# Order of SP's value loads and of POOL's second-sketch read for the last batch, in a polysketch attention and feed-forward kernel

## The chip, the cores and the metric

The kernel runs on one core of a Trainium2 chip. The metric is the device time of one execution in microseconds (us). The engines are named as in the profile: PE (TensorE), DVE (VectorE), ACT (ScalarE), POOL (GpSimd) and SP (SyncE, which here only issues transfers). Each engine works through its own list of instructions in order; what it waits for are semaphores that other engines or landed transfers raise.

## The reference

Four batches with four heads, a sequence of 1088, head dimension 32, sketch size 8; then a feed-forward layer with a squared ReLU over all 4352 tokens (d_model 128, d_ff 2048).

```
def phi(x):
    a = einsum('rd,bhsd->bhsr', S1, x)
    b = einsum('rd,bhsd->bhsr', S2, x)
    return einsum('bhsi,bhsj->bhsij', a, b).reshape(*x.shape[:-1], 64)
q_p, k_p = phi(q), phi(k)
kv  = einsum('bhsf,bhsd->bhfd', k_p, v);  z = sum(k_p, axis=2)
num = einsum('bhsf,bhfd->bhsd', q_p, kv)
den = einsum('bhsf,bhf->bhs', q_p, z)[..., None] + 1e-06
x   = (num / den) as (4352, 128)
out = square(maximum(x @ w_in, 0)) @ w_out
```

The feature map phi of a row is the outer product of two sketches of it, the first with S1, the second with S2: 8 x 8 = 64 features a head.

## The kernel before

The work is cut into 578 named operations, each a few instructions on one engine. A string, PLAN, holds all of them in one order written out in full, as `name:engine:buffers`; what an engine runs, it runs in the order in which its operations stand in PLAN. Waits follow from the data and the buffers that operations share.

Names carry the batch and a part. For batch b:

- **Loads** (on SP): ldk, ldq and ldv bring K, Q and V. V of one batch comes in five pieces, ldvb.0 to ldvb.4 (L494): four of 128 KB into `vin`, one small one into `vtl`. The weights come on POOL: w_in0, w_out0, w_in1, w_out1, w_in2, w_out2 (L377, L382), after a small copy called gate that waits for a value load.
- **Keys and values**: tk transposes K (DVE), ksk makes both sketches (PE), kr brings them into rows (DVE, L583), kp multiplies them to features (DVE, L591), vp copies V into rows with a one behind them (POOL, L527 and L530), kv multiplies features and values (PE, L654), in parts kvb.0 and kvb.1; vpb.0 needs all four large pieces of V. kve brings the result out of PSUM.
- **Queries of batches 0 and 1**: tq transposes (DVE), qr makes replicated sketches (PE, L727), qa and qp copy and multiply them (ACT L749, DVE L763), num, mx, tx and xe make the quotient and lay it out as x.
- **Queries of batches 2 and 3**: qr (PE, L859) makes both sketches of all heads, ab copies them to the tile `ab` (ACT). The denominator is worked out first, from zm, zt, zk, zb, dt and dr (DVE and PE); dx spreads its reciprocal (POOL, L891), and da (DVE, L896 and L897) multiplies it into the first sketch. The sketches are then written to a scratch tensor `scr` in device memory, each in four transfers on SP (L903): wrb.1.0 to wrb.1.3 is the second sketch, wrb.0.0 to wrb.0.3 the first, with the denominator in it. They are read back, spread over 128 partitions, in two halves of the sequence (0 and 544): rdA (SP, L918, two transfers) brings the first sketch into `qp`, rdB (L925, four transfers) the second into `Bq`, on POOL, but for rdB3.544 on SP. All halves are 544 KB. qp (DVE, L965) multiplies the two, num (PE, L982) makes x, xe copies it out of PSUM (L995).
- **Feed-forward**: ten stages n of 256 or 512 tokens. For each pair m of column tiles of d_ff: m1.n.m (PE, L1094) multiplies x by w_in, r.n.m takes the ReLU (ACT L1104, some on DVE L1106), g.n.m squares (DVE L1114, some on ACT L1112), m2.n.m (PE, L1128) adds the product with w_out. oe.n transposes the result (DVE, L1153; the last stage copies it, L1139), and four stores a stage and batch, st n.token.quarter, go out on SP (L1163, the last at L1144).
- **Heat** operations are matmuls of zeros ahead of the real work.

Stages of the feed-forward run between the attention of later batches: stages 1 to 4 are at work while batches 2 and 3 are prepared, and stage 6 needs xe3.0. Three PSUM tiles h0 to h2 of two banks each are shared by m1, sketches and num; four tiles r0 to r3 and four g0 to g3 hold what r and g make.

The SP list around the change, from PLAN with the other engines left out:

```
ldk3.0 ldv3.1 ldv3.4 ldq3.0 wr2.1.1 wr2.1.3 st0.0.0 wr2.1.2 wr2.1.0 ldv3.0 st1.256.3 ldv3.2 ldv3.3
wr2.0.0 wr2.0.3 wr2.0.2 wr2.0.1 rdA2.0 wr3.1.2 st2.768.3 wr3.1.1 rdA2.544 wr3.1.3 st1.256.1 wr3.1.0
st0.0.2 wr3.0.2 wr3.0.3 wr3.0.1 wr3.0.0 rdA3.0 rdA3.544 st3.1280.3 st2.1088.1 rdB3.544 ...
```

and the whole POOL list:

```
mk2 iota zc z0 SR gate vp0.0 kp0.7 w_in0 w_out0 w_in1 w_out1 w_in2 w_out2 S64 SKw z1 vp1.1 vp1.0
vp2.1 vp2.0 rdB2.0 dx2 vp3.0 vp3.1 rdB2.544 dx3 rdB3.0
```

mk2, iota, zc, z0, z1, SR, S64 and SKw are small constants and arranged sketch matrices; ident and zr on DVE are an identity and its sums.

Of the kernel before, what the change touches and what calls it, by code (L numbers as in the profile page):

```python
# [40 lines left out]
zero:DVE mk2:POOL ldk0.0:SP mkz:DVE mk:DVE S1:SP heat0:PE:o0 iota:POOL ident:DVE zr:DVE zc:POOL heat1:PE:o0 heat2:PE:o0 z0:POOL tk0.0:DVE heat3:PE:o0
heat4:PE:o0 heat5:PE:o0 heat6:PE:o0 S0:ACT ST:DVE SK:DVE ldk0.1:SP ldk0.2:SP tk0.1:DVE ldq0.0:SP heat7:PE:o0 ksk0.0:PE:a0 tq0.0:DVE ldv0.0:SP
ka0.0:ACT kp0.0:DVE ksk0.1:PE:h2.1 ka0.1:ACT kp0.4:DVE SR:POOL qr0.0:PE:h1.1:h1.0 qa0.0.0:ACT:A0 heat8:PE:o0 heat9:PE:o0 qp0.0.0:DVE ldv0.1:SP
ldv0.2:SP qa0.0.1:ACT:A1 ldv0.3:SP ldv0.4:SP ldq0.8:SP ldq1.0:SP heat10:PE:o0 heat11:PE:o0 heat12:PE:o0 gate:POOL qp0.0.1:DVE vp0.0:POOL kv0.0:PE:h0.1
ldk1.0:SP tq0.8:DVE qr0.1:PE:h2:h1 tq0.24:DVE kp0.7:POOL w_in0:POOL vp0.1:ACT qa0.1.1:ACT:A2 qp0.1.1:DVE qa0.1.0:ACT:A0 kv0.1:PE kv0.2:PE heat13:PE:o0
w_out0:POOL kve0.0:DVE num0.0:PE:a0 tq1.0:DVE w_in1:POOL qp0.1.0:DVE w_out1:POOL kve0.1:ACT kve0.2:ACT w_in2:POOL w_out2:POOL mx0.0:DVE:den0 tk1.1:DVE
qr0.2:PE:h1:h0 qa0.2.0:ACT:A1 qa0.2.1:ACT:A2 heat14:PE:o0 qp0.2.0:DVE num0.1:PE:h2 tx0.0:PE:a0 xe0.0:ACT S64:POOL heat15:PE:o0 heat16:PE:o0 ldv1.1:SP
tk1.0:DVE qp0.2.1:DVE mx0.1:DVE:den1 m1.0.0:PE:h1 r.0.0:ACT:r0 ksk1:PE:h0 heat17:PE:o0 g.0.0:ACT:g0 m1.0.1:PE:h1 r.0.1:ACT:r1 tx0.1:PE:a0 SKw:POOL
kr1:DVE kp1.4:DVE qr1.0:PE:h2:h0 ldv1.2:SP qa1.0.0:ACT:A0 qp1.0.0:DVE qa1.0.1:ACT:A1 xe0.1:ACT heat18:PE:o0 m2.0.0:PE:o0 m1.0.2:PE:h1 r.0.2:ACT:r2
g.0.1:DVE:g1 ldv1.3:SP ldv1.4:SP ldv1.0:SP ldk2.0:SP z1:POOL m1.0.3:PE:h2 r.0.3:ACT:r3 num0.2:PE:a0 tq1.12:DVE m1.1.4:PE:h1 m2.0.1:PE ldq2.0:SP  # L50
r.1.4:ACT:r0 m1.1.0:PE:h2 r.1.0:ACT:r1 g.0.2:DVE:g2 mx0.2:DVE:den2 g.0.3:DVE:g3 qp1.0.1:DVE m2.0.2:PE kp1.0:DVE vp1.1:POOL m1.1.1:PE:h1 tx0.2:PE:a0
xe0.2:DVE m2.0.3:PE r.1.1:ACT:r2 g.1.1:DVE:g0 ldv2.0:SP qr1.1:PE:h0:h2 vp1.0:POOL g.1.4:DVE:g1 m1.1.3:PE:h1 g.1.0:ACT:g2 ldv2.4:SP qa1.1.1:ACT:A2
r.1.3:ACT:r3 ldv2.1:SP kv1.0:PE:a0 oe0:DVE:osb0 qp1.1.1:DVE kv1.1:PE m1.1.2:PE:h1 m2.1.0:PE:o0 qa1.1.0:ACT:A0 m1.1.5:PE:h2 tq2.0:DVE qp1.1.0:DVE
st0.0.1:SP tk2.0:DVE ldv2.2:SP tk2.1:DVE kve1.0:ACT kve1.1:ACT m2.1.1:PE ldv2.3:SP r.1.2:ACT:r1 kve1.2:ACT g.1.2:DVE:g3 r.1.5:ACT:r2 m1.1.7:PE:h0
g.1.5:ACT:g2 vp2.1:POOL ldk3.0:SP num1.0:PE:a0 mx1.0:DVE:den0 qr2:PE:h1 ksk2:PE:h2 ldv3.1:SP tx1.0:PE:a0 ldv3.4:SP ldq3.0:SP r.1.7:ACT:r0 g.1.3:DVE:g0
m1.1.6:PE:h0 ab2:ACT wr2.1.1:SP xe1.0:ACT m2.1.2:PE r.1.6:ACT:r1 m1.2.3:PE:h1 wr2.1.3:SP r.2.3:ACT:r2 st0.0.0:SP kr2:DVE kp2.0:DVE g.1.7:ACT:g3
kp2.4:DVE m2.1.3:PE m1.2.4:PE:h2 r.2.4:ACT:r3 tk3.0:DVE vp2.0:POOL kv2.0:PE:a0 tk3.1:DVE qr1.2:PE:h0:h1 wr2.1.2:SP kv2.1:PE zm2:DVE wr2.1.0:SP
m2.1.4:PE qa1.2.0:ACT:A1 qp1.2.0:DVE zt2:PE:h2.1 zk2:DVE m2.1.5:PE qa1.2.1:ACT:A2 m1.2.0:PE:h0 g.1.6:ACT:g0 m2.1.6:PE m1.2.1:PE:h2 m2.1.7:PE ldv3.0:SP
qp1.2.1:DVE kve2:ACT zb2:PE:a0 r.2.0:ACT:r0 rdB2.0:POOL tq3.0:DVE g.2.0:ACT:g1 oe1:DVE:osb1 r.2.1:ACT:r1 dt2:DVE m1.2.2:PE:h1 r.2.2:ACT:r0 dr2:DVE
dx2:POOL num1.1:PE:h0.1 num1.2:PE:h0.0 g.2.1:ACT:g2 g.2.2:ACT:g0 mx1.1:DVE:den1 ksk3:PE:h2 kr3:DVE qr3:PE:h1 st1.256.3:SP ldv3.2:SP ab3:ACT  # L60
tx1.1:PE:a0 xe1.1:ACT ldv3.3:SP m2.2.0:PE:o0 da2:DVE m1.2.5:PE:h2 r.2.5:ACT:r1 m2.2.1:PE kp3.0:DVE wr2.0.0:SP m1.2.6:PE:h1 r.2.6:ACT:r0 wr2.0.3:SP
m2.2.2:PE g.2.3:DVE:g3 mx1.2:DVE:den2 g.2.5:DVE:g1 g.2.4:ACT:g2 vp3.0:POOL g.2.6:DVE:g0 kv3.0:PE:a0 m1.3.0:PE:h2 r.3.0:ACT:r2 m2.2.3:PE m1.2.7:PE:h1
wr2.0.2:SP kp3.4:DVE m1.3.2:PE:h0 vp3.1:POOL m2.2.4:PE m1.3.7:PE:h2 g.3.0:DVE:g3 r.2.7:ACT:r1 g.2.7:DVE:g2 m2.2.5:PE m1.3.1:PE:h1 r.3.2:ACT:r3
g.3.2:DVE:g1 r.3.1:ACT:r0 m2.2.6:PE r.3.7:ACT:r2 g.3.1:DVE:g0 kv3.1:PE m2.2.7:PE zm3:DVE oe2:DVE:osb2 m1.3.4:PE:h0 zt3:PE:h1.1 wr2.0.1:SP zk3:DVE
m1.3.5:PE:h2 kve3:ACT g.3.7:DVE:g2 r.3.4:ACT:r1 rdB2.544:POOL m2.3.0:PE:o0 zb3:PE:a0 rdA2.0:SP qp2.0:DVE r.3.5:ACT:r3 tx1.2:PE:h1.1 wr3.1.2:SP
xe1.2:ACT dt3:DVE dr3:DVE m1.3.3:PE:h0 r.3.3:ACT:r0 g.3.3:DVE:g3 m2.3.1:PE num2.0:PE:h2 xe2.0:ACT m1.3.6:PE:h1 g.3.4:ACT:g0 st2.768.3:SP m2.3.2:PE
wr3.1.1:SP m1.4.2:PE:h0 m1.4.0:PE:h2 m2.3.3:PE r.3.6:ACT:r2 r.4.0:ACT:r0 g.3.5:DVE:g1 dx3:POOL da3:DVE g.3.6:DVE:g3 m2.3.4:PE m1.4.1:PE:h1 m2.3.5:PE
rdA2.544:SP m1.4.4:PE:h2 wr3.1.3:SP r.4.2:ACT:r1 qp2.1:DVE st1.256.1:SP g.4.0:DVE:g0 m2.3.6:PE m2.3.7:PE r.4.1:ACT:r3 r.4.4:ACT:r2 oe3:DVE:osb3
g.4.1:DVE:g1 wr3.1.0:SP m1.4.3:PE:h0 g.4.2:DVE:g3 r.4.3:ACT:r0 num2.1:PE:h1 m1.4.5:PE:h2 m2.4.0:PE:o0 xe2.1:DVE g.4.3:DVE:g2 r.4.5:ACT:r3 m1.4.6:PE:h0
r.4.6:ACT:r1 st0.0.2:SP m2.4.1:PE m1.5.0:PE:h1 r.5.0:ACT:r0 g.4.5:DVE:g0 wr3.0.2:SP g.4.4:DVE:g1 m2.4.2:PE wr3.0.3:SP wr3.0.1:SP wr3.0.0:SP  # L70
rdB3.0:POOL m1.4.7:PE:h2 m2.4.3:PE r.4.7:ACT:r3 m1.5.3:PE:h0 g.5.0:DVE:g3 rdA3.0:SP m2.4.4:PE rdA3.544:SP m1.5.5:PE:h1 r.5.3:ACT:r2 m2.4.5:PE
r.5.5:ACT:r0 m1.5.1:PE:h2 g.4.6:DVE:g2 m2.4.6:PE m1.5.2:PE:h0 g.4.7:DVE:g1 st3.1280.3:SP r.5.1:ACT:r1 qp3.0:DVE m2.4.7:PE oe4:DVE:osb4 r.5.2:ACT:r3
g.5.1:DVE:g0 num3.0:PE:h1 m1.5.6:PE:h2 m2.5.0:PE:o0 g.5.2:DVE:g2 m1.5.4:PE:h0 m2.5.1:PE g.5.3:DVE:g1 xe3.0:ACT m1.6.0:PE:h1 m2.5.2:PE r.5.6:ACT:r1
r.5.4:ACT:r3 st2.1088.1:SP m1.5.7:PE:h2 rdB3.544:SP g.5.6:DVE:g3 g.5.5:DVE:g0 m2.5.3:PE r.6.0:ACT:r2 m1.6.1:PE:h0 st2.768.0:SP g.5.4:DVE:g2
r.5.7:ACT:r1 st3.1280.1:SP m2.5.4:PE st0.0.3:SP g.6.0:DVE:g1 st3.1280.2:SP m1.6.4:PE:h1 m2.5.5:PE st4.2176.3:SP r.6.1:ACT:r0 qp3.1:DVE g.5.7:DVE:g2
g.6.1:DVE:g0 m1.6.6:PE:h2 r.6.4:ACT:r3 m2.5.6:PE m1.6.2:PE:h0 st2.768.2:SP r.6.6:ACT:r2 m2.5.7:PE oe5:DVE:osb0 m1.6.3:PE:h1 st5.2304.3:SP num3.1:PE:h2
m2.6.0:PE:o0 r.6.2:ACT:r1 st2.1088.3:SP g.6.2:DVE:g3 r.6.3:ACT:r0 m1.6.7:PE:h0 st5.2304.0:SP xe3.1:ACT m2.6.1:PE g.6.6:DVE:g2 st5.2304.2:SP
st2.768.1:SP g.6.4:DVE:g1 st1.256.2:SP m1.6.5:PE:h1 m2.6.2:PE m1.7.1:PE:h2 r.6.5:ACT:r1 st1.256.0:SP r.7.1:ACT:r2 g.6.3:DVE:g0 m2.6.3:PE r.6.7:DVE:r3
st4.2176.0:SP st4.2176.2:SP m1.7.0:PE:h1 g.6.5:DVE:g3 m2.6.4:PE m1.9.1:PE:h0 m2.6.5:PE r.7.0:ACT:r0 g.7.0:ACT:g0 st4.1792.0:SP m1.7.2:PE:h2
r.7.2:ACT:r1 g.6.7:DVE:g1 st2.1088.0:SP m2.6.6:PE st4.1792.1:SP r.9.1:DVE:r3 m1.7.3:PE:h1 r.7.3:ACT:r0 g.7.1:DVE:g3 m2.6.7:PE st5.2304.1:SP  # L80
oe6:DVE:osb1 m1.7.4:PE:h0 st3.1280.0:SP st6.3264.2:SP m1.7.5:PE:h2 r.7.4:ACT:r2 g.7.2:DVE:g2 m2.7.0:PE:o0 m1.8.2:PE:h1 g.9.1:DVE:g1 r.7.5:ACT:r1
m2.7.1:PE st4.1792.2:SP st6.3264.0:SP r.8.2:ACT:r3 m1.7.7:PE:h0 m2.7.2:PE m1.7.6:PE:h2 g.7.4:DVE:g0 g.7.3:DVE:g3 m2.7.3:PE st6.3264.3:SP g.7.5:DVE:g2
r.7.7:ACT:r2 m1.8.0:PE:h1 r.7.6:DVE:r0 g.7.6:DVE:g3 m2.7.4:PE r.8.0:ACT:r1 m1.9.4:PE:a0 st4.2176.1:SP m2.7.5:PE g.7.7:ACT:g0 g.8.2:DVE:g2
st6.2816.3:SP m1.8.1:PE:h0 m2.7.6:PE st6.2816.1:SP r.8.1:DVE:r0 m1.9.0:PE:h2 g.8.0:ACT:g3 st4.1792.3:SP st6.2816.2:SP st6.2816.0:SP r.9.0:ACT:r2
st2.1088.2:SP st6.3264.1:SP m2.7.7:PE oe7:DVE:osb0 st7.3328.2:SP m1.9.2:PE:h1 st7.3328.3:SP m1.8.3:PE:h0 r.8.3:ACT:r3 r.9.2:ACT:r1 m2.8.0:PE:o0
g.8.1:DVE:g0 m2.8.1:PE st7.3328.1:SP st7.3328.0:SP m1.9.3:PE:h2.1 m2.8.2:PE r.9.3:ACT:r0 g.9.0:DVE:g3 g.8.3:DVE:g0 m2.9.0:PE:h0.1 g.9.2:DVE:g2
m2.8.3:PE oe8:DVE:osb3 m2.9.1:PE st8.3840.3:SP r.9.4:ACT:r2 m2.9.2:PE st8.3840.2:SP st8.3840.0:SP st8.3840.1:SP g.9.3:DVE:g3 m2.9.3:PE g.9.4:ACT:g0
m2.9.4:PE oe9:DVE:osb4 st9.0:SP
# [1124 lines left out]
```

## Time and profile before

| what | us |
|---|---|
| time, median of 3 runs | 112.12 (110.11, 112.12, 113.86) |
| the profiled execution, its own time | 109.22 |
| its span (first to last instruction of the program) | 107.4 |
| granted clock of PE in it | 0.99 |
| value loads ldv3.2 and ldv3.3 issued / landed | 44.11 to 45.23 / 50.2 |
| kv3.0 starts on PE | 51.02 |
| da3 ends on DVE | 64.24 |
| wr3.0.* issued / rdA3.0 issued | 64.27 to 65.97 / 69.35 |
| num3.0 starts on PE | 75.37 |
| last matmul ends / last store issued | 103.3 / 104.23 |

The page of the profile gives busy time by engine, the span in 40 slices, the transfers and the costliest groups. Beside it the trace is read through these views: the busy time of each engine in chosen stretches; the waits (who waited for whom, in total); the chain of waits that ended last, in order of time; and each engine's timeline. "SPq" and "POOLq" are what an engine's sequencer does, such as issuing a transfer; a transfer's landing is told apart from its issue.

### The profile page before, as it was taken

How to read it: one execution, taken by the hardware profiler on the slowest of the kernel's cores; microseconds unless marked ns; L12 is line 12 of the kernel's file. 1: busy time of each engine (PE TensorE's matmuls, PEld its weight loads, DVE VectorE, ACT ScalarE, POOL GpSimd, SP SyncE). 2: the span in 40 equal slices, each digit the busy share in tenths (PEclk: the TensorE clock that was granted, in tenths of full speed). 3: DMA queues.
4: the chain of work that ended last, by engine and by line, in shares of the span. 5: the costliest groups of instructions: out<-in, count | busy, mean ns of one | idle time of the engine just before them, and what ended most of it. 6: DMA issues, size and time to landing. Idle time of an engine off the chain costs nothing.

```text
span 107.4 us, 3577 instructions
## 1 busy us (share of the span) xinstructions
PE 96.3 (90%) x1418; PEld 56.4 (52%) x1433; DVE 93.9 (87%) x171; ACT 88.6 (83%) x126; POOL 28.6 (27%) x68
## 2 busy tenths in 40 slices
...
GB/s 60 228 237 214 335 141 150 263 228 221 117 56 264 82 261 51 131 195 65 107 184 157 130 161 112 148 185 243 202 132 1 43 109 71 59 87 45 98 40 58
DMA packets 26849, 15.23 MB, mean 142 GB/s; under 512 B 19536, under 2 KB 24144, under 8 KB 26832
## 3 DMA queue, kind: packets, MB, share of 16 engines
...
q8 instruction: 11, 0.18, 0.7%
...
## 4 chain that ended last, share of the span: by engine, by line
PE 40%; DVE 22%; ACT 11%; DMA 9%; issue 8%; SPq 5%; POOL 1%; POOLq 0%; ACTq 0%; DVEq 0%
PE o L1128 15%; PE h L1094 14%; ACT r L1104 10%; DVE g L1114 6%; DMA vin<-in_v_dram 5%; DMA qin<-in_q_dram 4%; PE h L727 3%; SPq L494 3%; DVE qp L763 2%; DVE kp L591 2%; PE a L654 2%; PE h L1123 2%; DVE osb L1153 2%; DVE qT L708 1%; PE h L982 1%
## 5 line engine op out<-in xcount | busy, mean ns | idle before, releaser
L1104 ACT ACTIVATE r<-h 128x1024 bf16<-128x1024 f32 x64 | 60.6, 1043 | 2.6 <-PE h L1094 1.2
L1094 PE MATMUL h<-xT,w_in 128*128 128x512 bf16 (+1 forms) x151 | 38.3, 347 | 0.7 <-ACT r L1104 0.2
L1114 DVE TENSOR_TENSOR g<-r 128x1024 bf16<-128x1024 bf16 (+1 forms) x55 | 37.2, 709 | 1.5 <-ACT r L1104 0.8
L1128 PE MATMUL o<-g,w_out 128*128 128x512 bf16 (+1 forms) x140 | 36.9, 355 | 0.7 <-issue 0.3
L1094 PEld LDWEIGHTS <-w_in 128*128 128x128 bf16 x160 | 17.4, 114 | 14.7 <-issue 3.7
L1128 PEld LDWEIGHTS <-w_out 128*128 128x128 bf16 x144 | 13.6, 98 | 12.1 <-issue 0.9
L1112 ACT ACTIVATE g<-r 128x1024 bf16<-128x1024 bf16 (+1 forms) x14 | 14.4, 1034 | 0.3
L527 POOL COPY vp<-vin 128x512 f32<-128x512 f32 x7 | 5.6, 809 | 19.2 <-DMA vin<-in_v_dram 12.8
L925 POOL DMA_DIRECT2D Bq<-scr x12 | 6.8, 582 | 8.1 <-DMA scr<-ab 8.0
L749 ACT COPY A<-h 128x256 f32<-128x256 f32 (+3 forms) x16 | 5.4, 397 | 3.9 <-PE h L727 3.4
L591 DVE TENSOR_TENSOR kp<-kt 128x1280 f32<-128x1280 f32 (+1 forms) x6 | 8.4, 1413 | 0.1
L763 DVE TENSOR_TENSOR qp<-h,A 128x256 f32<-128x256 f32 (+3 forms) x16 | 6.4, 421 | 2.1 <-ACT A L749 2.0
L363 PE MATMUL o<-zero 128*128 128x512 bf16 (+2 forms) x15 | 5.5, 495 | 1.4 <-DVE mk L278 1.2
L654 PE MATMUL a<-vp,kp 128*32 128x33 f32 x432 | 4.8, 198 | 2.0 <-POOL vp L527 1.5
L654 PEld LDWEIGHTS a<-vp,kp 128*32 128x32 f32 x432 | 4.2, 109 | 4.1 <-POOL vp L527 2.4
L1153 DVE STREAM_TRANSPOSE osb<-o 128x512 f32<-128x512 f32 (+1 forms) x9 | 5.9, 651 | 0.4 <-PE o L1128 0.3
L965 DVE TENSOR_TENSOR qp<-qp,Bq 128x1088 f32<-128x1088 f32 x4 | 5.1, 1286 | 1.1 <-DMA qp<-scr 1.1
L727 PE MATMUL h<-qT,SR 32*64 32x192 f32 (+2 forms) x176 | 5.8, 338 | 0.2 <-DVE qT L708 0.2
L708 DVE STREAM_TRANSPOSE qT<-qin 128x1088 f32<-128x1088 f32 (+5 forms) x7 | 5.6, 811 | 0.1
L1106 DVE TENSOR_SCALAR r<-h 128x1024 bf16<-128x1024 f32 x4 | 4.9, 1218 | 0.1
L530 POOL COPY vp<-vtl 32x128 f32<-32x128 f32 x6 | 4.2, 708 | 0.2
L363 PEld LDWEIGHTS <-zero 128*128 128x128 bf16 x19 | 2.0, 115 | 4.2 <-issue 2.6
...
## 6 DMA issues: line engine op xcount, KB each, us to landing
...
```

The costliest lines, as they stand in the source:

```text
L363: nc.tensor.matmul(tiles["o0"][:, 0:w], zero[:, 0:128], zero[:, 0:w], start=True, stop=True)
L591: (nc.vector if e == "DVE" else nc.gpsimd).tensor_tensor(out=kp[i][:, k0:k1].rearrange("p j h (x y) -> p (j h) x y", y=R), in0=v[:, :, 1, ...
L654: nc.tensor.matmul(t[p : p + KW, 33 * (h // 2) : 33 * (h // 2) + 33], kp[i][:, j, h, KW * f : KW * f + KW], vp[i][:, h, j, :], start=(j == ...
L727: nc.tensor.matmul(at(hb[h // 2])[lo : lo + 64, 512 * s + 256 * x : 512 * s + 256 * x + ns[s]], SR[32 * h : 32 * h + 32, x].rearrange("p x ...
L763: nc.vector.tensor_tensor(out=o, in0=pv, in1=av, op=ALU.mult)
L925: (nc.sync if e == "SP" else nc.gpsimd).dma_start(out=Bq[i][64 * m : 64 * m + 64, pr, s0:s1], in_=scr[i][1][8 * (2 * pr + m) : 8 * (2 * pr ...
L1094: nc.tensor.matmul(at(hb)[:, c : c + N], w_in[:, 512 * (ct // E) : 512 * (ct // E) + 512].rearrange("p (c e) -> p e c", e=E)[:, ct % E], x ...
L1104: nc.scalar.activation(o, s, ACTF.Relu)
L1112: nc.scalar.activation(at(gb)[:, 0 : W * N], r, ACTF.Square)
L1114: nc.vector.tensor_tensor(out=at(gb)[:, 0 : W * N], in0=r, in1=r, op=ALU.mult)
L1128: nc.tensor.matmul(at(ob)[:, 0:N], w_out[:, ct, :], at(gb)[:, N * w : N * w + N], start=(ct == 0), stop=(ct == CT - 1))
L1153: nc.vector.transpose(at(sbuf)[:, 0:N], at(ob)[:, 0:N])
```

## The change

There are two edits. In the code, a marker operation dx3.w is added: a memset on POOL of the first column of batch 3's first sketch in `ab`. Since the four writes wr3.0.* read that tile, the memset waits until they have landed. rdB3.0 depends on it and stands behind it on POOL.

```
                 sp = s0 > 0 and b == B - 1
-                o2 = add(f"rdB{b}.{s0}", {"SP" if sp else RD_B: (2.4, 3.2)}, f_b, (wrB or wr) + prev(b, "qprod"),
+                if s0 == 0 and b == B - 1 and not near:
+                    def f_w(e):
+                        nc.gpsimd.memset(ab[i][:, 0, 0:1], 0.0)
+                    after_wr = [add(f"dx{b}.w", {"POOL": (0.15, 0.2)}, f_w, wr)]
+                else:
+                    after_wr = []
+                o2 = add(f"rdB{b}.{s0}", {"SP" if sp else RD_B: (2.4, 3.2)}, f_b, (wrB or wr) + after_wr + prev(b, "qprod"),
                          dma=(0.6 if sp else 1.15) * dm, n=4, after=[o_rd[0][2]] if sp else [])
```

The PLAN string is replaced by another order of the same operations. Lines of it around the change, cut:

```
-m2.1.4:PE qa1.2.0:ACT:A1 qp1.2.0:DVE zt2:PE:h2.1 ... m2.1.7:PE ldv3.0:SP
-qp1.2.1:DVE kve2:ACT zb2:PE:a0 ... num1.1:PE:h0.1 ... qr3:PE:h1 st1.256.3:SP ldv3.2:SP ab3:ACT
-tx1.1:PE:a0 xe1.1:ACT ldv3.3:SP m2.2.0:PE:o0 da2:DVE ...
+wr2.1.1:SP zm2:DVE g.1.6:ACT:g3 ... zk2:DVE ldv3.3:SP ldv3.2:SP ldv3.1:SP ldv3.0:SP qa1.2.0:ACT:A2 kve2:ACT
...
-r.4.6:ACT:r1 st0.0.2:SP ... wr3.0.2:SP g.4.4:DVE:g1 m2.4.2:PE wr3.0.3:SP wr3.0.1:SP wr3.0.0:SP
-rdB3.0:POOL ... rdA3.0:SP m2.4.4:PE rdA3.544:SP ...
+wr3.0.0:SP wr3.0.2:SP ... wr3.0.1:SP m2.4.4:PE g.4.6:DVE:g2 ...
+wr3.0.3:SP dx3.w:POOL rdB3.0:POOL m2.4.5:PE rdA3.0:SP ... rdB3.544:SP rdA3.544:SP
```

The SP list then reads, from ldk3.0 on:

```
ldk3.0 wr2.1.0 ldq3.0 st0.0.0 wr2.1.3 st0.0.3 ldv3.4 wr2.1.2 wr2.1.1 ldv3.3 ldv3.2 ldv3.1 ldv3.0 st1.256.3
wr2.0.2 wr2.0.0 wr2.0.3 wr2.0.1 rdA2.0 wr3.1.3 wr3.1.1 wr3.1.2 st1.256.1 rdA2.544 st2.1088.0 wr3.1.0
st2.768.3 st1.256.0 wr3.0.0 wr3.0.2 wr3.0.1 wr3.0.3 rdA3.0 rdB3.544 rdA3.544 st0.0.2 ...
```

and the POOL list:

```
z1 SR z0 iota vp0.0 kp0.7 mk2 gate w_in0 w_out0 S64 w_in1 w_out1 w_in2 w_out2 vp1.1 SKw vp1.0 zc
vp2.0 vp2.1 rdB2.0 dx2 vp3.0 vp3.1 rdB2.544 dx3 dx3.w rdB3.0
```

On DVE, ident and zr move from ahead of the first transpose to behind tq0.8, ahead of tq0.24; between zm3 and da3 the order is zm3 oe2 zk3 qp2.0 dt3 dr3 g.3.3 xe1.2 da3 (before: zm3 oe2 zk3 g.3.7 qp2.0 dt3 dr3 g.3.3 g.3.5 da3), and ahead of qp3.0 it is r.4.7 g.4.5 g.4.7 g.4.6 g.5.3 g.5.0. On PE, m1.5.6 and m1.5.4 now stand ahead of num3.0. From DVE to ACT go g.3.1, xe2.1, g.5.1, g.6.7, g.9.3 and oe9; from ACT to DVE go xe1.2, r.4.7, r.5.4, g.7.0 and g.9.4. Apart from the marker no operation is added or removed. Other operations change places with near neighbours, and many change buffers of the same kind.

96 lines of the change are left out of this document (48 added, 48 removed).

## The prediction

> **What bounds the kernel now.** The page's head comes first, then the busy time by stage, the waits, the chain of waits, and the timelines of SP, POOL and DVE around the change.
>
> ```profile
> PE 96.3 (90%) x1418; PEld 56.4 (52%) x1433; DVE 93.9 (87%) x171; ACT 88.6 (83%) x126; POOL 28.6 (27%) x68
> ```
>
> No engine is the bound alone. The stages say where time is left (columns: stretch, sum; busy PE, PEld, DVE, ACT, POOL; granted clock; DMA share; GB/s):
>
> ```profile
> 17.00:27.00 10.00, 9.38 (x158) 6.82 (x166) 9.71 (x20) 8.96 (x13) 2.42 (x4) 1.00 0.94 224
> 49.00:57.00 8.00, 6.42 (x165) 3.55 (x166) 7.43 (x12) 6.68 (x8) 5.93 (x8) 1.00 0.48 132
> 66.00:75.40 9.40, 8.23 (x54) 3.61 (x54) 8.20 (x14) 9.40 (x11) 0.94 (x2) 1.00 0.75 194
> 75.40:90.00 14.60, 14.55 (x94) 6.94 (x96) 13.73 (x20) 13.92 (x19) 0.00 (x0) 1.00 0.45 91
> ```
>
> From 17 to 49 us DVE has almost no idle time (9.71 of 10 here, 10.90 of 11 from 27 to 38, 10.51 of 11 from 38 to 49), and from 75.4 us on PE has almost none. Two stretches are loose, 49 to 57 and 66 to 75.4. The waits name what is behind them (engine, line, waited for: us in total, times, longest):
>
> ```profile
> POOL vp L527 <- DMA vin<-in_v_dram: 12.8, 3, 8.2
> ...
> PE a L654 <- POOL vp L527: 1.5, 1, 1.5
> ...
> ACT r L1104 <- remote: 1.1, 1, 1.1
> DVE qp L965 <- DMA qp<-scr: 1.1, 1, 1.1
> ```
>
> The chain of waits shows the first hole step by step (start, us, what), and SP's timeline why it came:
>
> ```profile
> 44.80 5.41 DMA vin<-in_v_dram
> ...
> 50.35 0.62 POOL vp L527
> ...
> 51.02 0.77 PE a L654 x60
> ```
>
> ```profile
> 43.73 0.33 SPq L1163 DMA_DIRECT2D out_dram<-osb  x1
> 44.11 1.12 SPq L494 DMA_DIRECT2D vin<-in_v_dram  x2
> 48.09 1.92 SPq L903 DMA_DIRECT2D scr<-ab  x4
> 51.30 1.23 SPq L918 DMA_DIRECT2D qp<-scr  x2
> ...
> 64.27 1.70 SPq L903 DMA_DIRECT2D scr<-ab  x4
> 69.35 2.50 SPq L918 DMA_DIRECT2D qp<-scr  x4
> ```
>
> SP runs in order. Store st1.256.3 (43.73) waits for oe1, which ends at 43.70, and the last two value loads of batch 3 stand behind it. They land at 50.2, vp3.0 runs, and kv3.0 starts on PE at 51.02 after 1.48 us of idle PE; ACT is idle 1.15 us for the same reason. The second hole is at the end of these rows: the writes wr3.0 are issued from 64.27 to 65.97, but the read rdA3.0 that waits for them starts only at 69.35, 3.4 us later. The same four writes of batch 2 end at 50.01 and their reader starts at 51.30, 1.3 us later. What differs is POOL:
>
> ```profile
> 64.72 2.22 POOL L925 DMA_DIRECT2D Bq<-scr  x4 [1.88 <-DMA scr<-ab]
> ```
>
> ```profile
> 73.97 1.29 DVE L965 TENSOR_TENSOR qp<-qp,Bq 128x1088 f32<-128x1088 f32 x1 [1.13 <-DMA qp<-scr]
> ```
>
> rdB3.0 (544 KB) is asked for in the middle of the writes. DVE then sits idle 1.13 us for qp3.0, and num3.0 starts on PE at 75.37 after 0.90 us.
>
> **The change part by part.** The sum is made against the profiled execution: span 107.4, its own time 109.22, so 1.8 us lie around the span. The three runs shown have a median of 112.12 (110.11 to 113.86), 2.9 above it; I put the difference onto the median.
>
> *Value loads ahead of the store.* In the new SP order eleven transfers stand between ldk3.0 (31.5) and the last value load; the first of them needs ab2 (ACT, 35.10), and at 0.44 us an issue the last of the twelve is out by about 40.4. With the longest landing of this load in the stage (5.41) all are there by 46. POOL is then at dx2, which needs dr2 and ends at 46.14, so vp3.0 ends at 46.8. kv3.0 now waits for kp3.0 (DVE, ends 49.20) and its place on PE (m2.2.2 ends 49.54). The whole PE wait of 1.48 and the 1.15 of ACT go; late next is DVE's kp3.0. But DVE is dense until 55.96, so at once this buys only its next idle, 0.50 before g.3.1.
>
> *da3 comes earlier.* In before DVE goes from 55.96 to the end of da3, 64.24, in 8.28 us. The new order drops that 0.50, gives g.3.1 to ACT (0.61 by its spacing), puts g.3.7 (0.58) and g.3.5 (0.83) behind da3 and takes xe1.2 in (0.31, the row of the equal xe0.2). 8.28 - 0.50 - 0.61 - 0.58 - 0.83 + 0.31 = 6.07: da3 ends near 62.0 to 62.3 (POOL's dx3, 0.69, must fit in between).
>
> *wr3.0, then the mark, then rdB3.0.* Four writes: 1.70, to about 63.9. Landing: 1.3 (batch 2's row, no read under way) to 3.4 (batch 3's, with rdB3.0 under way). I take 1.3, since the new order has no read in flight there: rdA2.544 now stands ahead of the store st2.1088.0 and goes out some 4 us earlier. So the writes are there at 65.2 (67.3 at the worst). The mark dx3.w is a POOL memset of one column; POOL's memset rows are 0.10 to 0.21. Only rdB3.0 is behind it on POOL. rdB3.0's fourth issue starts at 65.4 + 1.66 = 67.0; this tile's landings are 3.2 / 3.5 / 5.6 (min, median, max), and as rdA3.0 and rdB3.544 now run beside it I take the upper half: there at 70.5 to 72.6 (74.7 at the worst). rdA3.0 is issued from 65.2 and is there by about 71.
>
> *Does qp3.0 wait?* In before DVE needs 8.61 us from da3 to 72.85. In the new order three more g (3 x 0.61) stand there, and r.4.7 (1.13) in place of xe2.1 (0.63): 10.9. From 62.1 DVE reaches qp3.0 at 73.0, after its data. So qp3.0 ends at 74.3, against 75.27. num3.0 starts at 74.4 if ACT lets it: ACT gains 1.15 at 51.2, takes on g.3.1 and xe2.1 and gives away r.4.7 and xe1.2 (+0.95 + 0.61 - 0.90 - 0.43 = +0.2), so r.5.5, which frees num3.0's buffer, ends at 74.4 to 74.9. I take 74.6.
>
> *The rest of the span.* PE has then done two more pairs (m1.5.6, m1.5.4; 2 x 0.43). It is ahead by 75.37 - 74.6 + 0.87 = 1.6 us. In before PE needs 27.95 us from there to the end without a gap. It stays the bound: ACT loses r.5.4 to DVE (0.9), and DVE has about 2 us of small gaps there. Bounds of the gain: 0.4 (qp3.0 at 74.7) to 2.4 (both PE waits, 1.48 + 0.90).
>
> *The front.* POOL's order moves too. The weights' issues came at 10.46 to 13.36; now mk2 and gate stand ahead of them (0.38 + 0.18) and S64 (1.01) among them, so w_in0 is 0.6 and w_in2 about 1.7 us later. w_in2 was issued at 12.84 and landed 7.4 later, at 20.2; m1.0.2 used it at 21.05. It lands between 20.8 (the queue is full, DMA share 0.94, so a later issue costs less) and 22.0, and m1.0.2 and g.0.2 behind it are late by 0 to 0.95. DVE is dense there, so it goes through to the end. I take the middle, 0.45. zc and SKw move behind vp1.1 and vp1.0; POOL was idle 6.27 us there, so zc is free, and SKw (0.59) makes kv1.0 0.4 late, hidden as num1.0's reader on DVE was 0.3 behind it: 0 to 0.3, taken as 0. ident and zr (1.0) go into DVE's idle 1.59 before qp0.1.1: nothing. At the end oe9 goes from DVE (0.42) to ACT (0.37 for the equal copy): nothing, st9.0 stands behind four stores as before. Other exchanges of places stay within 0.3 either way.
>
> Sum: -1.6 + 0.45 = -1.15, to 108.1 for the profiled execution and 112.12 - 1.15 = **111.0** for the median.
>
> **The rivals.**
>
> *More than the sum (109.0).* The runs shown lie 0.9 to 4.6 us above the profiled one, and waits on DMA are what varies between equal programs. If the two holes are deeper there, the new order, with 3 us to spare at kv3.0, takes out more. With no cost in front and both PE waits gone the gain is 2.4, and 0.7 more if each hole is half deeper in DMA time: 112.12 - 3.1 = 109.0. Against it: qp3.0 has under 2 us to spare.
>
> *The holes are covered anyway (112.2).* DVE, dense to 55.96, keeps the pace; the only idle it had is 0.50 and 1.13. If r.5.5 and DVE come to qp3.0 as late as before and the front costs 0.95, then -0.87 (the two pairs) + 0.95 = 0.1 over before.
>
> *Slower: rdB3.0 becomes the last (114.1).* Before, rdB3.0 was issued 4.6 us ahead of rdA3.0; now rdA3.0, rdB3.0, rdB3.544 and rdA3.544 (4 x 544 KB) are asked for within 5 us. At the 194 GB/s of this stage 2.18 MB take 11.2 us; if they share evenly, all end late, near 65.4 + 11.2 = 76.6, and the two that qp3.0 needs near 76.2. That is 3.15 after DVE is ready: -1.15 + 3.15 = +2.0. It decides from 73.0 + 1.15 = 74.2 on. Against it: two of the four are needed first, slices of this stage show up to 243 GB/s, and rdB3.0 needs half the bytes. The Trainium skill (DMA: Bandwidth & Descriptors, "Queues, rings and completion order") speaks for this rival: each DMA engine takes turns between the queues that have work, packet by packet, so a read on POOL's queue and one on SP's slow each other. The trace agrees in the one place that shows it: wr3.0 took 3.4 us beside rdB3.0 against 1.3 for wr2.0.
>
> **How the numbers follow.** Forecast 0.45 (109.9 to 111.8 on the median), more 0.25, covered 0.14, slower 0.16. The low end of the range takes in most of the "more" case, the high end the near half of the slow one: 108.2 to 113.8; the likeliest case's own range is 109.9 to 111.8. A measurement of this kernel tells about 2% (2.2 us) from no change. Faster by more: the "more" case and a little of the forecast, 0.31; within: 0.52; slower by more: the far part of the slow case and mishaps of order, 0.17.
>
> **What would show it.** kv3.0 starts by 49.7 with no wait on POOL (right) or still waits (wrong). rdA3.0 starts within 1.5 us of the last wr3.0 (right) or over 3 (then the mark bought nothing). No DVE wait before qp3.0; a wait on DMA Bq<-scr over 1.2 us is the slow rival. Idle ACT before r.0.2 near 21.9 is the front's cost. PE without gaps from num3.0 to its end, which falls about 1.2 us earlier.

## The result and the profile after

| | before | after |
|---|---|---|
| time, median (range, runs), same chip and hour | 111.12 (109.51 to 113.86, 4) | 113.47 (112.81 to 113.80, 4) |
| ratio after/before, 95% interval | | 1.033 (1.022 to 1.043): slower |
| profiled execution: own time / span | 109.22 / 107.4 | 113.15 / 111.3 |
| granted clock in it | 0.99 | 0.972 |
| kv3.0 starts on PE | 51.02 | 50.29 |
| da3 ends on DVE | 64.24 | 62.81 |
| last wr3.0 issued / rdA3.0 issued | 65.97 / 69.35 | 64.85 / 66.10 |
| rdB3.0 first issue / last landing | 64.72 / 69.99 | 66.83 / 76.02 |
| qp3.0 starts on DVE / num3.0 on PE | 73.97 / 75.37 | 76.10 / 77.49 |
| last matmul ends / last store issued | 103.3 / 104.23 | 106.3 / 108.16 |

The profiled execution of before is one of its quicker ones, so the two spans differ by 3.9 us where the medians differ by 2.35; ratios here compare undisturbed executions alone. The page's first line of after, and then the four stretches that were shown of before (columns as there: stretch, sum; busy PE, PEld, DVE, ACT, POOL; granted clock; DMA share; GB/s):

```profile
PE 99.7 (90%) x1433; PEld 56.4 (51%) x1433; DVE 93.0 (84%) x170; ACT 89.3 (80%) x127; POOL 27.3 (24%) x69
```

```profile
17.00:27.00 10.00, 9.99 (x150) 6.84 (x146) 9.20 (x20) 8.71 (x12) 2.56 (x8) 1.00 0.95 234
49.00:57.00 8.00, 7.67 (x173) 4.15 (x172) 7.70 (x13) 8.00 (x9) 1.84 (x4) 1.00 0.64 170
66.00:75.40 9.40, 8.87 (x53) 3.92 (x52) 7.67 (x12) 9.31 (x14) 2.32 (x5) 1.00 0.80 201
75.40:90.00 14.60, 12.51 (x77) 5.27 (x78) 12.77 (x17) 10.88 (x15) 0.00 (x0) 0.88 0.33 69
```

PE's busy time rose by 3.4 us though its matmuls are the same (both have 1433 weight loads; before's profile lacks a few records of matmuls); part of that is the clock, as a matmul takes longer when it is low, and the last stretch shows 0.88. The loose stretch 49 to 57 has closed (PE 7.67 of 8, before 6.42). The last one, which had no gap in before (14.55 of 14.60), has opened on three engines at once. The waits of after say for what (engine, line, waited for: us in total, times, longest; lines from L925 on are six further down than in before):

```profile
POOL ab L933 <- DMA scr<-ab: 4.5, 1, 4.5
...
PE h L988 <- issue: 2.6, 1, 2.6
DVE qp L971 <- DMA out_dram<-osb: 2.4, 1, 2.4
ACT xT L1001 <- PE h L988: 2.4, 1, 2.4
```

The first is the marker, which waits for the writes as it is meant to. The other three are one wait seen from three engines: qp3.0 on DVE, num3.0 behind it on PE, xe3.0 behind that on ACT. The DVE line names a store, but qp3.0 needs none: a wait is put down to what came last by the profile, and that can be the wrong transfer. Of qp3.0's inputs the last to land, by the landings in the trace, is the fourth part of rdB3.0, at 76.02. The timelines of SP, POOL and DVE in after show how it came to be late:

```profile
39.85 2.92 SPq L494 DMA_DIRECT2D vin<-in_v_dram  x4
44.10 0.33 SPq L1169 DMA_DIRECT2D out_dram<-osb  x1
...
62.84 2.01 SPq L903 DMA_DIRECT2D scr<-ab  x4
66.10 1.17 SPq L918 DMA_DIRECT2D qp<-scr  x2
67.31 2.57 SPq L925 DMA_DIRECT2D Bq<-scr  x4
69.99 1.19 SPq L918 DMA_DIRECT2D qp<-scr  x2
...
98.33 9.73 SPq L1169 DMA_DIRECT2D out_dram<-osb  x16
108.16 0.63 SPq L1150 DMA_DIRECT2D out_dram<-osb  x1
```

```profile
46.73 1.17 POOL L527 COPY vp<-vin 128x512 f32<-128x512 f32 x2
...
66.30 0.10 POOL L933 MEMSET ab<- 128x1 f32 x1 [4.48 <-DMA scr<-ab]
66.83 2.22 POOL L925 DMA_DIRECT2D Bq<-scr  x4 [0.44 <-issue]
```

```profile
76.10 1.29 DVE L971 TENSOR_TENSOR qp<-qp,Bq 128x1088 f32<-128x1088 f32 x1 [2.38 <-DMA out_dram<-osb]
```

The upper rows are the half of the change that worked: the value loads are issued by 42.8, ahead of the store at 44.10, and vp3.0 runs at 46.7 instead of 50.35. The writes wr3.0 end at 64.85, and rdA3.0 follows 1.25 us later. But rdA3.0 (66.10), rdB3.0 (66.83, on POOL), rdB3.544 (67.31) and rdA3.544 (69.99) are now in flight together. The DMA columns of two stretches of after (last two: share of the 16 DMA engines, GB/s) show that they fill the DMA engines:

```profile
68.00:72.00 4.00, 4.00 (x20) 1.98 (x19) 4.00 (x7) 3.95 (x8) 1.06 (x2) 1.00 0.85 235
72.00:76.00 4.00, 2.87 (x13) 1.09 (x11) 1.67 (x3) 4.00 (x5) 0.00 (x0) 1.00 0.99 229
```

The parts of rdB3.0 land at 72.04, 73.03, 75.33 and 76.02, the last of them 7.6 us after its own issue. Then something follows that the prediction didn't have at all. PE's timeline in after, and the clock by stretch:

```profile
73.74 1.13 PE L1100 MATMUL h<-xT,w_in 128*128 128x512 bf16 x4
77.49 0.89 PE L988 MATMUL h<-qp,kvF 64*32 64x272 f32 x16 [2.62 <-issue]
78.32 1.89 PE L1134 MATMUL o<-g,w_out 128*128 128x512 bf16 x4
80.00 1.06 PE L1100 MATMUL h<-xT,w_in 128*128 128x512 bf16 x2
...
82.36 0.59 PE L1100 MATMUL h<-xT,w_in 128*128 128x512 bf16 x2
```

```profile
75.00:78.00 3.00, 0.51 (x16) 0.21 (x16) 1.90 (x3) 1.08 (x2) 0.00 (x0) 0.98 0.57 162
78.00:79.00 1.00, 1.00 (x10) 0.28 (x3) 1.00 (x3) 0.57 (x2) 0.00 (x0) 0.50 0.21 44
79.00:80.00 1.00, 1.00 (x4) 0.30 (x2) 0.90 (x2) 0.97 (x2) 0.00 (x0) 0.50 0.04 5
80.00:81.00 1.00, 1.00 (x4) 0.45 (x3) 1.00 (x2) 0.00 (x0) 0.00 (x0) 0.50 0.46 80
82.00:84.00 2.00, 2.00 (x11) 0.98 (x10) 1.59 (x3) 2.00 (x4) 0.00 (x0) 1.00 0.40 67
```

PE is idle for 2.62 us; 0.4 us after it starts again the granted clock falls to 0.50 and stays there from 77.9 to 81.3, 3.4 us. Two matmuls of the same shape take 1.06 us at 80.00 and 0.59 at 82.36. From num3.0 at 77.49 to 81.50 PE does what takes 0.62 + 4 x 0.433 = 2.35 us at the full clock in 4.01: 1.66 lost.

So the 3.9 us between the two spans add up like this: PE is ready for num3.0 at 74.87, where in before, with the two pairs that now stand ahead (2 x 0.43), it would have been 74.47 + 0.87 = 75.34: -0.47. The wait is 2.62 instead of 0.90: +1.72. The clock: +1.66. The last store starts 1.45 after oe9 instead of 0.45, with oe9 0.05 sooner behind the last matmul: +0.95. It stands behind sixteen stores that SP issues without a pause from 98.33 on. Other work: +0.07. Together +3.93.

### The profile page after: what moved, and what is told of

It reads as the page before. It is cut to its first block, busy times and chain, and to the rows that moved or that the text cites. A ratio compares the mean times of both kernels' runs of the same rounds, so it can differ in the third digit from the quotient of the medians.

```text
span 111.3 us, 3601 instructions
## 1 busy us (share of the span) xinstructions
PE 99.7 (90%) x1433; PEld 56.4 (51%) x1433; DVE 93.0 (84%) x170; ACT 89.3 (80%) x127; POOL 27.3 (24%) x69
## 4 chain that ended last, share of the span: by engine, by line
PE 42%; DVE 26%; ACT 12%; issue 7%; SPq 4%; DMA 4%; ACTq 0%; DVEq 0%
PE o L1134 16%; PE h L1100 15%; ACT r L1110 8%; DVE g L1120 7%; DVE kp L591 5%; DMA qin<-in_q_dram 4%; PE a L654 3%; DVE kt L583 2%; DVE qp L763 2%; SPq L494 2%; PE h L988 2%; DVE qT L708 2%; ACT g L1118 2%; DVE xs L1057 2%; PE h L727 1%
## 5 line engine op out<-in xcount | busy, mean ns | idle before, releaser
L1110 ACT ACTIVATE r<-h 128x1024 bf16<-128x1024 f32 (+1 forms) x62 | 59.5, 1029 | 2.4 <-PE h L1100 2.0
L1100 PE MATMUL h<-xT,w_in 128*128 128x512 bf16 (+1 forms) x158 | 39.8, 352 | 0.0
L1134 PE MATMUL o<-g,w_out 128*128 128x512 bf16 (+1 forms) x144 | 38.9, 364 | 0.3 <-DVE g L1120 0.2
L1120 DVE TENSOR_TENSOR g<-r 128x1024 bf16<-128x1024 bf16 (+1 forms) x53 | 34.4, 680 | 2.0 <-PE o L1134 1.2
L1118 ACT ACTIVATE g<-r 128x1024 bf16<-128x1024 bf16 (+1 forms) x16 | 16.6, 1040 | 0.2
L925 POOL DMA_DIRECT2D Bq<-scr x12 | 6.8, 578 | 7.1 <-DMA scr<-ab 6.6
L363 PE MATMUL o<-zero 128*128 128x512 bf16 (+2 forms) x19 | 6.3, 471 | 1.2 <-DVE mk L278 1.2
L1112 DVE TENSOR_SCALAR r<-h 128x1024 bf16<-128x1024 f32 x6 | 7.3, 1219 | 0.0
L727 PE MATMUL h<-qT,SR 32*64 32x192 f32 (+2 forms) x176 | 6.3, 339 | 0.4 <-DVE ident L328 0.4
L988 PE MATMUL h<-qp,kvF 64*32 64x272 f32 x64 | 3.0, 421 | 2.6 <-issue 2.6
L727 PEld LDWEIGHTS h<-qT,SR 32*64 32x64 f32 x176 | 3.6, 131 | 1.6 <-issue 0.9
```

The source lines that it names most:

```text
L727: nc.tensor.matmul(at(hb[h // 2])[lo : lo + 64, 512 * s + 256 * x : 512 * s + 256 * x + ns[s]], SR[32 * h : 32 * h + 32, x].rearrange("p x ...
L925: (nc.sync if e == "SP" else nc.gpsimd).dma_start(out=Bq[i][64 * m : 64 * m + 64, pr, s0:s1], in_=scr[i][1][8 * (2 * pr + m) : 8 * (2 * pr ...
L1100: nc.tensor.matmul(at(hb)[:, c : c + N], w_in[:, 512 * (ct // E) : 512 * (ct // E) + 512].rearrange("p (c e) -> p e c", e=E)[:, ct % E], x ...
L1110: nc.scalar.activation(o, s, ACTF.Relu)
L1112: nc.vector.tensor_scalar_max(o, s, 0.0)
L1118: nc.scalar.activation(at(gb)[:, 0 : W * N], r, ACTF.Square)
```

## The experiments

The theory after this profile: the order's other moves are right and worth what the prediction said, the marker is what costs, because it sends rdB3.0 into the three reads on SP, and two things come on top, the clock after PE's idle time and the stores at the end. The main rivals: the new order itself costs the time (its front or its end), or rdB3.0 is slow on POOL whatever runs beside it. No experiment changes what is computed: e4 puts zeros where num3.0 writes afterwards, the others change only waits, order and, in e6, the queue of one read.

**e1: the new order without the marker.**

```
-wr3.0.3:SP dx3.w:POOL rdB3.0:POOL m2.4.5:PE rdA3.0:SP ...
+wr3.0.3:SP rdB3.0:POOL m2.4.5:PE rdA3.0:SP ...
```

> The changed kernel without the marker; all else as in it. Theory 1 (the marker): rdB3.0 goes out near 62 instead of 66.8 and lands by 69; wr3.0 land beside it in about 3 us, so rdA3.0 goes out near 67.5 and lands near 72.5; qp3.0 starts at 73.7 without a wait or up to 0.7 late, PE idles under 1 us at num3.0 and its clock stays full. 3 us less than the changed kernel: ratio to before about 1.00, time near 110.5 where before shows 111. Theory 2 (the rest of the order: 0.9 us late in front, 0.95 at the last store): the marker costs little, since rdA3.0 then lands last: under 1 us less, ratio about 1.025.

Measured: 109.16 us (108.61 to 109.76), before beside it 111.08 (109.42 to 113.93); ratio 0.994 (0.983 to 1.004). That is 4.3 us less than after by the medians. SP's, POOL's and PE's timelines of e1:

```profile
63.49 2.01 SPq L903 DMA_DIRECT2D scr<-ab  x4
68.67 1.17 SPq L918 DMA_DIRECT2D qp<-scr  x2
69.89 2.48 SPq L925 DMA_DIRECT2D Bq<-scr  x4
72.47 1.18 SPq L918 DMA_DIRECT2D qp<-scr  x2
```

```profile
62.97 2.22 POOL L925 DMA_DIRECT2D Bq<-scr  x4 [0.50 <-DMA out_dram<-osb]
```

```profile
75.84 0.69 PE L982 MATMUL h<-qp,kvF 64*32 64x272 f32 x16 [0.33 <-ACT r L1104]
```

What the marker removes comes back: the writes, which end at 65.49, are seen only at 68.67, 3.2 us later, as rdB3.0 runs beside them. Yet num3.0 starts 1.65 us earlier than in after, though e1 was 0.65 behind at the end of da3 (63.46). rdB3.0 has 5 us almost to itself and lands at 69.14; rdA3.0, issued 2.6 us later than in after, lands at 73.03, only 0.3 us later than after's 72.73. So the marker brought rdA3.0's landing 0.3 us forward and put rdB3.0's off by 6.9. The order is not what made the kernel slow: the marker is.

**e2: the marker alone, in the order of before.**

```
-rdB3.0:POOL m1.4.7:PE ...
+dx3.w:POOL rdB3.0:POOL m1.4.7:PE ...
```

> Before with the marker alone, in front of rdB3.0 on POOL. Theory 1: the four writes land near 67.3 instead of 69.35, rdB3.0 goes out at 67.5 instead of 64.7 and, beside rdA3.0 and rdA3.544, lands near 75 to 76; qp3.0 starts 1 to 2 us later than 73.97, PE idles 2 to 3 us at num3.0, its clock falls to half behind that: 2 to 4 us slower, ratio 1.02 to 1.035. Theory 2: nothing (ratio within 0.995 to 1.005), as rdA3.0 lands earlier by the 2 us that rdB3.0 lands later.

Measured: 115.11 us (114.01 to 117.11); ratio 1.039 (1.023 to 1.055). The writes' landing falls to 1.76 us, rdB3.0 takes 8.2 us from its first issue to its last landing (70.72 to 78.94), and PE's timeline has the same pair of rows as after's:

```profile
80.42 1.17 PE L988 MATMUL h<-qp,kvF 64*32 64x272 f32 x16 [3.08 <-issue]
81.51 1.04 PE L1100 MATMUL h<-xT,w_in 128*128 128x512 bf16 x2
```

The marker costs about as much in another order: 3.9% here, and after's 113.47 is 3.9% above e1's 109.16. This execution had a second stall, at 49 to 57 us, long before the marker.

**e3: the value loads alone, in the order of before.**

```
-qr3:PE:h1 st1.256.3:SP ldv3.2:SP ab3:ACT tx1.1:PE:a0 xe1.1:ACT ldv3.3:SP m2.2.0:PE:o0
+qr3:PE:h1 ldv3.2:SP ab3:ACT tx1.1:PE:a0 xe1.1:ACT ldv3.3:SP st1.256.3:SP m2.2.0:PE:o0
```

> Before with store st1.256.3 moved behind the last value load of batch 3 on SP, nothing else. Both theories: kv3.0 starts at about 49.6 instead of 51.02 and PE's 1.48 us of idle go. Theory 1 expects a gain of 0.5 to 1.0 us (DVE's idle of 0.50 and what ACT and PE run ahead), ratio 0.99 to 0.995. Theory 2 expects none, 0.998 to 1.002: the gain is given back at qp3.0, whose data come no earlier than da3 allows.

Measured: 112.03, 108.38, 112.31 and 110.50 us, too far apart for a verdict against 111.08. In the profiled one the hole is gone (kv3.0 at 50.11, stretch 49 to 57 with PE busy 8.00 of 8.00), but the next stretch is worse:

```profile
57.00:66.00 9.00, 6.89 (x41) 2.90 (x41) 6.53 (x14) 6.25 (x10) 1.85 (x4) 0.83 0.51 124
```

With vp3.1 done early, POOL asks for rdB2.544 at 48.84, into the writes and reads of batch 2, and qp2.0 starts at 60.47 instead of 58.74. It is the collision of batch 3 one batch earlier. After has it too, at a lower price: rdB2.544 is asked for at 48.63, among the writes wr2.0 (48.22 to 49.93), the read rdA2.0 follows 3.2 us after the last of them (1.3 in before), and qp2.0 waits 0.32 us, where it waits 2.28 in e3. The prediction has no term for this. Whether it costs as much in the other executions of e3 is not shown.

**e4: after, with PE kept busy.** Eight matmuls of zeros go into num3.0's own PSUM tile ahead of its real ones, which start afresh.

```
-                def f_num(e, nb=nb, t0=t0):
+                def f_num(e, nb=nb, t0=t0, warm=8 if (b, g) == (3, 0) else 0):
+                    for _ in range(warm):
+                        nc.tensor.matmul(at(nb)[:, 0:512], zero[:, 0:128], zero, start=True, stop=True)
```

> The changed kernel with eight matmuls of zeros (512 columns) into num3.0's own PSUM tile ahead of its real ones; the real ones overwrite them. They run while PE would be idle, from about 75.2 to 76.9. Theory 1 with the clock as part of the loss: the granted clock stays at 1.00 from 78 to 81.3, the eight matmul pairs there take 0.43 us each instead of 0.85, and the kernel is 1.3 to 1.7 us faster than the changed one; ratio to before about 1.018. If the clock falls for another reason than PE's idle time, it falls here too and the time is that of the changed kernel.

Measured: 112.03 us (109.97 to 112.39, median of four), 1.4 us less than after's 113.47. All four lie below all four of after (112.81 to 113.80), but they spread too far to give the gain a size. PE's timeline and the stretch behind it:

```profile
75.83 1.89 PE L985 MATMUL h<-zero 128*128 128x512 bf16 x8 [0.32 <-ACT r L1112]
78.72 0.69 PE L990 MATMUL h<-qp,kvF 64*32 64x272 f32 x16 [1.01 <-DVE qp L971]
79.35 1.04 PE L1136 MATMUL o<-g,w_out 128*128 128x512 bf16 x4
```

```profile
78.00:82.00 4.00, 3.28 (x29) 1.49 (x30) 3.90 (x6) 2.48 (x4) 0.00 (x0) 1.00 0.49 105
```

num3.0 starts later than in after (78.72; rdB3.0 landed at 77.30 here), yet the clock stays at 1.00 and four matmuls take 1.04 us where after's took 1.89. The second loss is PE's idle time itself, not num3.0 or the matmuls behind it.

**e5: after, with the second halves asked for later.** rdB3.544 and rdA3.544 move behind the store st4.2176.3, which waits for oe4, so that rdA3.0 alone runs beside rdB3.0.

```
-... r.5.1:ACT:r3 g.5.0:DVE:g3 rdB3.544:SP rdA3.544:SP
+... r.5.1:ACT:r3 g.5.0:DVE:g3
-... g.5.5:DVE:g2 st4.2176.3:SP m1.6.1:PE:h0
+... g.5.5:DVE:g2 st4.2176.3:SP rdB3.544:SP rdA3.544:SP m1.6.1:PE:h0
```

> The changed kernel with its marker, but rdB3.544 and rdA3.544 on SP behind store st4.2176.3, which waits for oe4 and so for qp3.0. rdB3.0 then shares the transfers' engines with rdA3.0 alone. Theory 1 (rdB3.0 is late because it takes turns with SP's three reads): rdB3.0's last part lands within 5 us of its first issue, near 72 (76.0 in the changed kernel), qp3.0 starts without a wait at 73 to 74, PE's clock stays full; the second half then lands at 80 to 82 and may cost up to 1.5 us at num3.1: 1.5 to 3.5 us less than the changed kernel, ratio 0.995 to 1.015. Rival (POOL's own queue is slow after the marker, whoever runs beside it): rdB3.0 still lands at 75 or later, and the time is that of the changed kernel or more, ratio 1.03 to 1.045.

Measured: 115.16 us (115.09 to 116.64), before beside it 109.60; ratio 1.062 (1.048 to 1.076). DVE's and SP's timelines of e5, and two of its stretches:

```profile
74.36 1.29 DVE L971 TENSOR_TENSOR qp<-qp,Bq 128x1088 f32<-128x1088 f32 x1 [0.35 <-DMA Bq<-scr]
...
85.56 1.29 DVE L971 TENSOR_TENSOR qp<-qp,Bq 128x1088 f32<-128x1088 f32 x1 [4.36 <-DMA qp<-scr]
```

```profile
76.67 2.50 SPq L925 DMA_DIRECT2D Bq<-scr  x4
79.27 1.18 SPq L918 DMA_DIRECT2D qp<-scr  x2
```

```profile
68.00:72.00 4.00, 4.00 (x20) 1.90 (x20) 4.00 (x7) 3.95 (x8) 1.34 (x3) 1.00 1.01 269
72.00:74.00 2.00, 1.95 (x9) 0.93 (x9) 1.94 (x4) 2.00 (x3) 0.00 (x0) 1.00 0.17 43
```

The first half goes the theory's way, though not as far as forecast (within 5 us, near 72): the same four transfers on POOL, issued 0.3 us later than in after, land at 74.28 instead of 76.02, qp3.0 waits 0.35 instead of 2.38, and the DMA engines are done by about 73. The kernel as a whole got slower, against the forecast: the second halves, asked for from 76.67 on, make qp3.1 wait 4.36, PE stands idle 3.92 before num3.1, and the clock is low again behind it (0.69 from 86 to 90). The experiment puts one number on the sharing: rdB3.0 takes 9.2 us from first issue to last landing in after and 7.2 here, so the two later reads cost 2.0. It also shows that rdA3.0 alone still costs some, as it took 5.3 in before and 6.2 in e1, with only small writes beside it. The DMA packets in the traces tell sharing from a slow queue. Those of rdB3.0 run on POOL's queue for 3.2 us in before, 3.5 in e1, 5.1 in e5 and 6.9 in after, and in these times 63, 119, 441 and 1035 KB move on SP's queue. From the first issue to the first packet it is 1.4 us in before, e5 and after alike (1.9 in e1), so POOL's own start is not slower behind the marker.

**e6: no marker, and rdB3.0 on SP behind rdA3.0**, so that one queue orders all four.

```
-wr3.0.3:SP dx3.w:POOL rdB3.0:POOL m2.4.5:PE rdA3.0:SP ...
+wr3.0.3:SP m2.4.5:PE rdA3.0:SP rdB3.0:SP ...
```

> The changed kernel without the marker and with rdB3.0 issued by SP, right behind rdA3.0 and ahead of rdB3.544 and rdA3.544: it waits for the writes of the first sketch as with the marker, but is ahead of the second half in the same queue. Theory 1: rdA3.0 and rdB3.0 (1.09 MB) land by 72.5 to 73.5, qp3.0 waits 0 to 0.5 us, no clock drop; the time is that of the kernel without the marker, ratio 0.99 to 1.0. The rival of any wait for the writes being too late, whatever queue it is on: rdB3.0 lands after 75, ratio over 1.02.

Measured: 110.74 us (110.19 to 111.33), ratio 1.018 (1.006 to 1.031). The two transfers of rdA3.0 are issued at 67.79, 1.47 after the last write, and then eight in a row:

```profile
69.01 4.95 SPq L925 DMA_DIRECT2D Bq<-scr  x8
```

qp3.0 starts at 75.64, 11.35 after da3, where DVE's own work is 10.9. rdB3.0 is asked for 2.2 us later than in after (0.7 later counted from da3, which ends at 64.29 here), and DVE still waits only about 0.5: the second halves stand behind it in the same queue, not beside it in another. It beats after, but it is slower than forecast (0.99 to 1.0) and loses to leaving rdB3.0 early (e1, 108.61 to 109.76). In the profiled executions num3.0 starts 1.2 us later than in e1, and 0.8 of that is there at da3 already, so the waits are not the whole of the difference.

**e7: e1 with eight stores earlier.** Stores of stages 2 to 5 that stood behind st6.3264.2, which waits for oe6, go ahead of it.

```
-... st4.2176.2:SP m2.6.7:PE oe6:DVE:osb1 st6.3264.2:SP ... st3.1280.3:SP ... st5.2304.2:SP st2.768.2:SP ...
+... st4.2176.2:SP st3.1280.3:SP st5.2304.2:SP st2.768.2:SP st5.2304.0:SP st4.1792.1:SP st2.768.0:SP st3.1280.0:SP st4.1792.2:SP m2.6.7:PE oe6:DVE:osb1 st6.3264.2:SP ...
```

> The changed kernel without the marker, and with eight stores of stages 3 to 5 moved ahead of the first store of stage 6 on SP, into about 5 us in which SP only waits for oe6. Theory (SP's backlog of stores holds the last store): the last store goes out within 0.5 us of oe9's end instead of 1.0 us after it, 0.5 us less than the same kernel with the stores where they were; ratio to before 0.985 to 0.99. Rival (the last store's wait is that for its own four predecessors): no difference, 0.993.

Measured: 108.43 us (107.69 to 109.50, ten runs), before beside it 109.60 (108.29 to 112.96); ratio 0.999 (0.994 to 1.004). SP's end in e1, and then in e7:

```profile
96.88 7.46 SPq L1163 DMA_DIRECT2D out_dram<-osb  x14
104.44 0.63 SPq L1144 DMA_DIRECT2D out_dram<-osb  x1
```

```profile
97.55 5.05 SPq L1163 DMA_DIRECT2D out_dram<-osb  x9
102.69 0.63 SPq L1144 DMA_DIRECT2D out_dram<-osb  x1
```

In e1 SP issues the fourteen stores one after the other, 0.53 us each. In e7 nine are left and SP pauses 0.85 us among them, until oe8 has ended, so that it has caught up. The last one starts 0.28 us after oe9 instead of 1.02. The 0.74 is what was forecast at the store; that it shortens the kernel is not shown, as the ratio is not below e1's 0.994 and missed both forecasts. By its median this is the quickest version of the study, 5 us under after; by the ratios to before (0.999 and 1.033), which ran quicker beside e7 than beside after, it is 3.3% or some 3.7 us. Against before it is not told apart by the interval; its slowest run of ten is 109.50, where before reached 112.96.

**e8: e1 with two value loads back behind the store.** ldv3.1 and ldv3.0 follow st1.256.3 again.

```
-... zk2:DVE ldv3.3:SP ldv3.2:SP ldv3.1:SP ldv3.0:SP qa1.2.0:ACT:A2 ... oe1:DVE:osb1
+... zk2:DVE ldv3.3:SP ldv3.2:SP qa1.2.0:ACT:A2 ... oe1:DVE:osb1 st1.256.3:SP ldv3.1:SP ldv3.0:SP
```

> The changed kernel without the marker, and with the last two value loads of batch 3 back behind store st1.256.3 on SP, as in before. If the move of the loads is what gains: kv3.0 starts 1.5 to 2 us later than with the loads ahead, PE is idle 1 to 2 us there, in some executions with a drop of the clock behind it, and the time goes up by 0.7 to 2.5 us, to 110 to 111.7, with a wider spread. If the rest of the order gains: within 0.3 us of 109.2.

Measured: 111.51 us (110.59 to 112.57), ratio 1.022 (1.008 to 1.037). POOL's and PE's timelines of e8:

```profile
51.27 1.85 POOL L527 COPY vp<-vin 128x512 f32<-128x512 f32 x2 [2.77 <-DMA vin<-in_v_dram]
```

```profile
52.15 0.76 PE L654 MATMUL a<-vp,kp 128*32 128x33 f32 x64 [0.41 <-POOL vp L527]
```

kv3.0 waits for POOL again. e1 and e8 ran beside different runs of before; by their ratios (0.994 and 1.022) e8 is about 2.9% slower, by the medians 2.35 us, and all four of its runs lie above all four of e1. How much of that the loads are worth is not shown. In the profiled executions num3.0 starts 1.32 us later than in e1 (77.16 against 75.84), but kv2.0, ahead of every load that was moved, already starts 0.89 later (39.69 against 38.80). At kv3.0 itself the loads cost 0.4: it starts 0.52 us after kp3.0 ends, in e1 0.15. The first edit does what it was made for, as the wait on POOL goes with it and comes back without it; what it is worth in time stays open.

## Why the prediction was wrong

It said 111.0, and within 2% as the likeliest; it is 113.47, and slower by 3.3% (2.2 to 4.3). Against its sum for the profiled execution 5.1 us are missing: 2.4 because num3.0 starts at 77.49 and not at 75.05 (74.6 and 0.45 for the front), 1.66 for the clock, 0.95 for the last store and 0.07 of other work. By its own steps:

- **Value loads ahead of the store: right.** kv3.0 starts at 50.29 after 0.33 of idle PE, waiting for kp3.0 and no longer for POOL (said: by 49.7; the kernel was 0.9 late by then). e8 undoes it and the wait is back. What that is worth at the end is not shown.
- **da3 earlier: right.** 62.81 (said 62.0 to 62.3), with the same 0.9 us of lateness in it. From there DVE needed 10.91 to be ready for qp3.0, as said (10.9); r.5.5 ended at 75.14 (said 74.4 to 74.9).
- **The front: not shown as a cost of the order.** r.0.2 starts at 22.72 against 21.85. But it starts at 22.93 and 23.14 in e2 and e3, which have the order of before there, and at 22.09 to 24.35 in the kernels with the new one. In after the delay came with 0.57 us of idle PE inside num0.1; its cause stays open.
- **"wr3.0, then the mark, then rdB3.0": here it failed.** The first number holds: the writes are seen 1.25 us after the last is issued (1.2 to 1.8 in e2, e4, e5 and e6, also without rdB3.0 beside them; 2.6 to 3.6 in e1, e3, e7 and e8, with it). Batch 2's row was not quite without a read, as a part of rdB2.0 landed at 49.87 and the value loads at 50.21, but 1.3 held. The second number does not hold: rdB3.0 was to be there at 70.5 to 72.6, at worst 74.7, from rows (3.2 / 3.5 / 5.6) that were taken with one such read in flight at a time. The 5.6 itself was a part of rdB2.0 that landed beside two value loads. With three reads of the same size beside it the longest was 7.6 and the end 76.02. The text named the sharing, priced it in the slower rival (qp3.0 at 76.2; measured 76.10), set the point from which that decides (74.2), and then kept its own rows' maximum and gave the rival 0.16. The rival's arithmetic, bytes in flight over the stage's rate, was the better row: 4 x 544 KB were asked for within 5 us, and when they are served in turns, the two needed first end near the last. (544 KB are 544 x 1024 bytes, so its 11.2 us should read 11.5.) The Trainium skill (DMA: Bandwidth & Descriptors, "Queues, rings and completion order") says each DMA engine alternates between the queues that have work, packet by packet. The runs agree that reads on the two queues slow each other: rdB3.0 took 9.2 us beside three reads on SP's queue, 7.2 beside one and 5.3 to 6.2 beside small writes.
- **What the mark buys was not asked.** rdA3.0 was issued 2.6 us earlier than in e1 and landed 0.3 us earlier, as it now shared too. In before the writes were held up by rdB3.0, but the half that was read meanwhile was needed as well. The 3.4 us were not idle time of the DMA engines (in e1 rdB3.0's packets run from 64.9 to 68.4, and rdA3.0 is issued at 68.67), they were the price of rdB3.0.
- **"In before PE needs 27.95 us from there to the end without a gap": missing a term.** PE's own work behind num3.0 took 1.73 longer, of which 1.66 is the halved clock. The rival's 114.1 was near the result partly by chance: its wait was 3.15, the real one on DVE 2.38, and the clock and the stores filled the difference.
- **"st9.0 stands behind four stores as before: nothing": wrong by about 1 us.** It stands behind sixteen that SP issues one after the other. e7 took away 0.74 of e1's 1.02.

Left open: whether e6 gains by the one queue or by the order in it, as it moves both together; and what the first edit alone is worth (e3 and e8).
